# Retention and two matmul layers on one core: the decay moved from the chunks to the tokens

## The chip, the cores and the metric

One Trainium2 chip, one NeuronCore. The metric is the device time of one execution in microseconds, the median of several runs. The lower it is, the better.

## What is computed

The first part is attention with a decaying state, for 4 sequences of 768 tokens and 8 heads of width 64:

```python
gamma = 1.0 - 2.0 ** (-5.0 - np.arange(H))
for t in range(S):
    state = gamma * state + outer(k[t], v[t])      # 64 x 64 for each head
    y[t] = (1 / sqrt(D)) * q[t] @ state
x = y                                              # 3072 tokens x 512
h = ((x @ w1) * (x @ w2)) @ w3 @ w_out             # 512 -> 1024 -> 1024 -> 512
z = h @ w_in                                       # 512 -> 2048
out = (z * sigmoid(1.702 * z)) @ moe2_w_out        # 2048 -> 512
```

The weights arrive as float64 and q, k, v as float32. The output is float32, 3072 x 512.

## The kernel before

**Stage 0** (chunks) goes over 24 chunks of 128 tokens, six to a sequence. For a chunk, TensorE makes the scores k·q of all heads (L193, 8 matmuls, which the trace shows as 16 passes), VectorE multiplies them by a table that holds the causal mask, the decay and the scale (L217, two instructions, each for one head of every pair), and TensorE multiplies v by the result into the output y (L259). From the second chunk of a sequence on, TensorE adds the state times q (L269). q is scaled for that by GpSimd (L206). The state itself is renewed once in a chunk: GpSimd scales k by the decay to the end of the chunk (L209), TensorE multiplies it with v into PSUM (L228), GpSimd multiplies the old state by the decay of a whole chunk (L241), and VectorE adds the two (L247, two instructions on 64 partitions each; L251, a copy, in the first chunk of a sequence). ScalarE copies y to SBUF (L283) and issues its DMA to memory (L284). Of the first four chunks y stays on the chip, split into a high and a low part (L145 on ScalarE, L146 on VectorE).

**Weights** run beside this. A weight is loaded in 72 pieces of 128x512 float64 (512 KB), and `tick()` moves the pieces on by a step: it fetches pieces (L88, on SyncE's queue), and for three pieces at different stages ScalarE takes a scaled absolute value (L107), VectorE makes a float32 of the two words in four instructions (L110, L111, L112, L115), ScalarE rounds it to the high part (L103) and GpSimd subtracts to get the low part (L119). `TICKS` says how many steps a chunk takes: 1 in chunks 0 to 12, 2 in chunks 13 to 18, 1 in the last five. From chunk 12 on, TensorE also multiplies w3 by w_out, in halves of 12 matmuls (`mix`, `HALVES`: 16 halves in all); each second half ends in ScalarE and VectorE instructions (L303, L304).

**Stages 1 and 2** are the layers, over 6 blocks of 512 tokens. Every product is three matmuls (L129 to L131: high·high, high·low, low·high). In stage 1 a block has 8 steps f of 24 + 12 matmuls. Between the 24 and the 12, ScalarE copies one product (L382), VectorE multiplies it by the other (L383), ScalarE rounds (L364) and VectorE subtracts (L365). In the last four steps the next block is loaded and split (L145, L146). Block 0 takes two weight steps for each f (four at f = 0), block 5 two. Stage 2 has 16 steps of 24 matmuls; in its first block each has one weight step.

Each engine works through its instructions in the order in which the program issues them (`tc.manual_schedule()`). In a chunk c that is:

```python
load_qk(c + 2); load_kv(c + 2)
scale_qk(c + 1); scores(c + 1)
if HALVES[c] > 0: mix_half()
if TICKS[c] > 1: tick()
updates(c)
if HALVES[c] > 1: mix_half()
outputs(c); next_state(c)
masked(c + 1)
if TICKS[c] > 0: tick()
```

The PSUM tiles for y and for the state's update have one buffer each, those for the scores two each.

Of the kernel before, what the change touches and what calls it, by code (L numbers as in the profile page):

```python
# [7 lines left out]
F32 = mybir.dt.float32  # L8
# [3 lines left out]
ALU = mybir.AluOpType  # L12
# [24 lines left out]
def tile_kernel(  # L37
# [10 lines left out]
    cq: bass.AP,  # L48
    ck: bass.AP,
    cg: bass.AP,  # L50
# [39 lines left out]
    def tick():  # L90
        """A step of the weights' pieces, each of which is at another stage."""
# [26 lines left out]
        if 0 <= l < len(pieces):  # L118
            nc.gpsimd.tensor_tensor(lo, whole, hi.bitcast(F32), ALU.subtract)  # L119
# [31 lines left out]
    with tc.manual_schedule():  # L151
        with (
# [32 lines left out]
            sc, pt, qs, ks, us = {}, {}, {}, {}, {}  # L185

            def scores(c):
                pair = []
                for j in range(2):
                    t = ps0.tile([P, NP, P], F32, tag=f"s{j}", bufs=2, name=f"sc{j}")  # L190
                    r = slice(j * D, (j + 1) * D)
                    for p in range(NP):
                        nc.tensor.matmul(  # L193
                            t[:, p, :],
                            qkt[c][r, 1, p, :],
                            qkt[c][r, 0, p, :],
                            start=True,
                            stop=True,
                        )
                    pair.append(t)  # L200
# [20 lines left out]
            def updates(c):  # L221
                """What the chunk adds to the state."""
                if c % NCK == NCK - 1:
                    return
                us[c] = ps0.tile([P, NP, D], F32, tag="u", name="u")
                for p in range(NP):
                    for j in range(2):
                        nc.tensor.matmul(  # L228
                            us[c][j * D : (j + 1) * D, p, :],
                            ks[c][:, 2 * p + j, :],  # L230
                            kvt[c, 1][:, 2 * p + j, :],
                            start=True,
                            stop=True,
                        )

            def next_state(c):
# [15 lines left out]
                del us[c]  # L252

            def outputs(c):
                y = ps0.tile([P, NP, P], F32, tag="y", name="y")
                first = c % NCK == 0
                for p in range(NP):
                    for j in range(2):
                        nc.tensor.matmul(  # L259
                            y[j * D : (j + 1) * D, p, :],  # L260
                            kvt[c, 1][:, 2 * p + j, :],
# [5 lines left out]
                if not first:  # L267
                    for p in range(NP):
# [3 lines left out]
                            qs[c][:, p, :],  # L272
# [5 lines left out]
                t = slice(t0, t0 + P)  # L278
                if i == order[0]:
# [283 lines left out]
```

## Time and profile before

| | |
|---|---|
| time, median of 3 runs | 1127.29 us (1125.37 to 1127.29) |
| span of the profiled execution | 1124.6 us |
| TensorE busy | 1082.3 us, 96% of the span |
| VectorE busy | 540.0 us |
| ScalarE busy | 312.0 us |
| GpSimd busy | 164.0 us |
| mean granted TensorE clock | 0.988 |

The span runs from the first to the last instruction, and the profiled execution's own time is the span and a few microseconds around it. PE is TensorE, PEld its weight loads, DVE VectorE, ACT ScalarE, POOL GpSimd. "L112" is line 112 of the kernel. "Busy" counts an instruction from its start to its end, whatever it did in between.

### The profile page before, as it was taken

Reading aid. Unit: us, or ns where it says so; the run is one execution under the profiler, and the core shown is the slowest. Engines: PE = TensorE matmul, PEld = TensorE weight load, DVE = VectorE, ACT = ScalarE, POOL = GpSimd, SP = SyncE. Lnnn points to the kernel's source line nnn. Section 1 sums busy time; section 2 is a strip of 40 time slices with the busy share of each in tenths; the row PEclk is TensorE's granted clock in tenths of the full one; section 3 lists DMA queues with packets and bytes.
Section 4 is the critical chain, followed back from the end, with each engine's and each line's share of the span. In section 5 each row is a group of like instructions: output and inputs, shape, how many; then the busy total and the mean of one; then the engine's idle time right before and its main releaser. Section 6 shows DMA issues by size and latency. Waiting matters only on the chain.

```text
span 1124.6 us, 13473 instructions
## 1 busy us (share of the span) xinstructions
PE 1082.3 (96%) x5472; PEld 891.4 (79%) x5472; DVE 540.0 (48%) x744; ACT 312.0 (28%) x534; POOL 164.0 (15%) x134
## 2 busy tenths in 40 slices
PE   7879998998999999999998999999999999999998
PEld 6767777876888888888876888888888888888886
DVE  4999998994222222223897823223223223223222
ACT  1223323342122112212344423222223223223222
POOL 4666563320000000000322200000000000000000
PEclk9899999998999999999998999999999999999999
DMA  9887764432011010101443101002002001001001
GB/s 364 275 291 248 239 237 143 145 132 75 10 35 50 20 57 19 57 10 62 173 132 132 38 18 59 0 10 66 1 9 67 1 1 62 14 1 44 13 1 38
DMA packets 45183, 93.94 MB, mean 84 GB/s; under 512 B 4417, under 2 KB 14657, under 8 KB 45121
## 3 DMA queue, kind: packets, MB, share of 16 engines
q1 hardware_dynamic: 34560, 87.84, 22.8%
q10 hardware_dynamic: 10560, 5.24, 1.6%
q8 instruction: 43, 0.70, 0.2%
q14 instruction: 20, 0.16, 0.0%
HBM read 75.24 MB, written 17.83 MB: 83 GB/s over the span
## 4 chain that ended last, share of the span: by engine, by line
PE 76%; DVE 20%; issue 2%; ACT 1%; DMA 1%; ACTq 0%; DVEq 0%
PE psm L130 13%; PE psm L129 13%; PE psm L131 13%; PE acc L129 11%; PE acc L131 11%; PE acc L130 11%; DVE x L112 6%; DVE x L110 4%; DVE x L111 3%; DVE pt L217 2%; DVE x L115 2%; PE sc L193 1%; PE y L259 1%; DVE tmp L383 1%; PE y L269 1%
## 5 line engine op out<-in xcount | busy, mean ns | idle before, releaser
L129 PE MATMUL psm<-xh,wh 128*128 128x512 f32 x768 | 300.4, 391 | 8.3 <-ACT xh L145 8.3
L130 PE MATMUL psm<-xl,wh 128*128 128x512 f32 x768 | 300.3, 391 | 0.0
L131 PE MATMUL psm<-xh,wl 128*128 128x512 f32 x768 | 299.8, 390 | 0.0
L441 DVE TENSOR_TENSOR tmp<-tmp,psm 128x512 f32<-128x512 f32 x96 | 65.9, 686 | 262.5 <-ACT tmp L440 262.5
L129 PEld LDWEIGHTS psm<-xh,wh 128*128 128x128 f32 x768 | 144.9, 189 | 39.4 <-ACT xh L145 9.2
L130 PEld LDWEIGHTS psm<-xl,wh 128*128 128x128 f32 x768 | 144.7, 188 | 30.9 <-DVE xl L146 1.0
L131 PEld LDWEIGHTS psm<-xh,wl 128*128 128x128 f32 x768 | 144.9, 189 | 30.0
L119 POOL TENSOR_TENSOR wl<-x,wh 128x512 fp32r<-128x512 f32 x72 | 94.3, 1310 | 473.0 <-ACT wh L103 470.0
L364 ACT CAST hh<-tmp 128x512 fp32r<-128x512 f32 x144 | 89.3, 620 | 222.5 <-DVE tmp L383 130.1
L131 PE MATMUL acc<-wh,hl 128*128 128x512 f32 x384 | 149.5, 389 | 0.0
L129 PE MATMUL acc<-wh,hh 128*128 128x512 f32 x384 | 149.5, 389 | 0.0
L130 PE MATMUL acc<-wl,hh 128*128 128x512 f32 x384 | 149.4, 389 | 0.0
L365 DVE TENSOR_TENSOR hl<-tmp,hh 128x512 fp32r<-128x512 f32 x144 | 99.6, 692 | 98.9 <-ACT hh L364 98.9
L440 ACT ACTIVATE tmp<-psm 128x512 f32<-128x512 f32 x96 | 57.2, 596 | 272.9 <-PE psm L131 272.8
L383 DVE TENSOR_TENSOR tmp<-tmp,psm 128x512 f32<-128x512 f32 x48 | 32.9, 685 | 165.7 <-PE psm L131 165.7
L129 PEld LDWEIGHTS acc<-wh,hh 128*128 128x128 f32 x384 | 72.0, 188 | 15.3 <-ACT hh L364 0.4
L131 PEld LDWEIGHTS acc<-wh,hl 128*128 128x128 f32 x384 | 72.0, 188 | 15.3 <-DVE hl L365 0.4
L130 PEld LDWEIGHTS acc<-wl,hh 128*128 128x128 f32 x384 | 72.2, 188 | 14.9
L112 DVE SCALAR_TENSOR_TENSOR x<-raw,x 128x512 int32<-128x512 int32 x72 | 81.1, 1127 | 2.5
L129 PE MATMUL acc<-hh,wh 128*128 128x512 f32 x192 | 76.5, 399 | 4.1 <-ACT hh L364 4.1
L130 PE MATMUL acc<-hl,wh 128*128 128x512 f32 x192 | 76.6, 399 | 1.0 <-DVE hl L365 0.8
L131 PE MATMUL acc<-hh,wl 128*128 128x512 f32 x192 | 75.7, 394 | 0.0
(47 smaller groups left out, 967.8 us busy)
## 6 DMA issues: line engine op xcount, KB each, us to landing
raw<-in_w_dram SPq DMA_DIRECT2D x32, 512.0 KB, 4.4
qkt<-in_qk_dram SPq DMA_DIRECT2D x24, 512.0 KB, 6.5
raw<-in_wo_dram SPq DMA_DIRECT2D x24, 512.0 KB, 4.9
raw<-in_wi_dram SPq DMA_DIRECT2D x16, 512.0 KB, 3.7
k<-in_kv_dram SPq DMA_DIRECT2D x24, 256.0 KB, 6.2
v<-in_kv_dram SPq DMA_DIRECT2D x24, 256.0 KB, 6.1
yd<-st SPq DMA_DIRECT2D x24, 256.0 KB, 2.4
xr<-yd SPq DMA_DIRECT2D x24, 256.0 KB, 3.1
```

The lines of the kernel that those rows point to most:

```text
L110: nc.vector.tensor_scalar(x, x, LEAST, MOST, ALU.max, ALU.min)
L111: nc.vector.tensor_scalar(bits, bits, 3, None, ALU.logical_shift_left)
L112: nc.vector.scalar_tensor_tensor(bits, raw[:, :, 0], 29, bits, ALU.logical_shift_right, ALU.bitwise_or)
L119: nc.gpsimd.tensor_tensor(lo, whole, hi.bitcast(F32), ALU.subtract)
L129: nc.tensor.matmul(ps, wh, xh, start=start, stop=False, skip_group_check=True)
L130: nc.tensor.matmul(ps, wh, xl, start=False, stop=False, skip_group_check=True)
L131: nc.tensor.matmul(ps, wl, xh, start=False, stop=stop, skip_group_check=True)
L364: nc.scalar.copy(hi, t)
L365: nc.vector.tensor_tensor(lo, t, hi.bitcast(F32), ALU.subtract)
L383: nc.vector.tensor_tensor(t, t, pb, ALU.mult)
L440: nc.scalar.activation(t, ps, AF.Sigmoid, scale=ALPHA)
L441: nc.vector.tensor_tensor(t, t, ps, ALU.mult)
```

## The change

The decay is split into one factor for each key token, which goes onto v, and one for each query token, which goes onto y, both relative to the middle of the sequence. Then the state needs no decay of its own:

- v is multiplied by its factor on VectorE (`scale_v`); q and k are used as they come (L206 and L209 are gone).
- The mask holds only zeros and ones, the same for all heads (64 KB, where there were 512 KB).
- The updates of a sequence accumulate in one PSUM tile. ScalarE copies the two diagonal parts to SBUF after each chunk. GpSimd's product (L241) and VectorE's sum (L247, L251) are gone.
- y is multiplied by its factor on VectorE, into SBUF, where ScalarE copied it before. The factors come in six tables of 256 KB, one loaded in each of the first chunks.
- The low part of a weight piece is subtracted on VectorE.
- The scores of a pair's two heads alternate, where all first heads came before all second ones.
- The loads ahead of the first chunk come in another order.

```diff
         if 0 <= l < len(pieces):
-            nc.gpsimd.tensor_tensor(lo, whole, hi.bitcast(F32), ALU.subtract)
+            nc.vector.tensor_tensor(lo, whole, hi.bitcast(F32), ALU.subtract)
...
             load_qk(0)
-            mask = p0.tile([P, 2, NP, P], F32, name="mask")
+            mask = p0.tile([P, 1, P], F32, name="mask")
             nc.sync.dma_start(mask, cmask)
+            dv = p0.tile([P, NCK, H, 1], F32, name="dv")
+            nc.sync.dma_start(dv, cv)
+            load_kv(0)
             load_qk(1)
-            dk = p0.tile([P, H, 1], F32, name="dk")
-            nc.sync.dma_start(dk, ck)
-            load_kv(0)
-            dq = p0.tile([P, NP, P], F32, name="dq")
-            nc.sync.dma_start(dq, cq)
+            dy = []
+            def load_dy():
+                t = p0.tile([P, NP, P], F32, name=f"dy{len(dy)}")
+                nc.sync.dma_start(t, cy[:, len(dy)])
+                dy.append(t)
+            load_dy()
             load_kv(1)
-            gc = p0.tile([P, NP, 1], F32, name="gc")
-            nc.sync.dma_start(gc, cg)
...
             def scores(c):
...
-                for j in range(2):
-                    t = ps0.tile([P, NP, P], F32, tag=f"s{j}", bufs=2, name=f"sc{j}")
-                    r = slice(j * D, (j + 1) * D)
-                    for p in range(NP):
+                for p in range(NP):
+                    for j in range(2):
+                        r = slice(j * D, (j + 1) * D)
                         nc.tensor.matmul(
-                            t[:, p, :],
+                            pair[j][:, p, :],
...
-            def scale_qk(c):
-                if c % NCK:
-                    qs[c] = p0.tile([P, NP, P], F32, tag="qs", bufs=2, name="qs")
-                    nc.gpsimd.tensor_tensor(qs[c], qkt[c][:, 0], dq, ALU.mult)
-                if c % NCK < NCK - 1:
-                    ks[c] = p0.tile([P, H, D], F32, tag="ks", bufs=2, name="ks")
-                    nc.gpsimd.tensor_tensor(
-                        ks[c], kvt[c, 0], dk.to_broadcast([P, H, D]), ALU.mult
-                    )
+            def scale_v(c):
+                vs[c] = p0.tile([P, H, D], F32, tag="vs", bufs=3, name="vs")
+                nc.vector.tensor_tensor(
+                    vs[c],
+                    kvt[c, 1],
+                    dv[:, c % NCK].to_broadcast([P, H, D]),
+                    ALU.mult,
+                )
...
-                    nc.vector.tensor_tensor(t, sc[c][j], mask[:, j], ALU.mult)
+                    nc.vector.tensor_tensor(
+                        t, sc[c][j], mask.to_broadcast([P, NP, P]), ALU.mult
+                    )
...
             def updates(c):
-                us[c] = ps0.tile([P, NP, D], F32, tag="u", name="u")
+                if n == 0:
+                    us[i] = ps0.tile([P, NP, D], F32, tag="u", name="u")
                 for p in range(NP):
                     for j in range(2):
                         nc.tensor.matmul(
-                            us[c][j * D : (j + 1) * D, p, :],
-                            ks[c][:, 2 * p + j, :],
-                            kvt[c, 1][:, 2 * p + j, :],
-                            start=True,
+                            us[i][j * D : (j + 1) * D, p, :],
+                            kvt[c, 0][:, 2 * p + j, :],
+                            vs[c][:, 2 * p + j, :],
+                            start=(n == 0 and p == 0),
...
             def next_state(c):
                 new = state[(c + 1) % 2]
-                if c % NCK:
-                    nc.gpsimd.tensor_tensor(
-                        new, state[c % 2], gc.to_broadcast([P, NP, P]), ALU.mult
-                    )
                 for j in range(2):
                     r = slice(j * D, (j + 1) * D)
-                    if c % NCK:
-                        nc.vector.tensor_tensor(
-                            new[r, :, r], us[c][r], new[r, :, r], ALU.add
-                        )
-                    else:
-                        nc.vector.tensor_copy(new[r, :, r], us[c][r])
+                    nc.scalar.copy(new[r, :, r], us[c // NCK][r])
...
             def outputs(c):
...
-                            qs[c][:, p, :],
+                            qkt[c][:, 0, p, :],
...
+                x = p0.tile([P, KD, P], F32, tag="xb", bufs=3, name="xb")
+                nc.vector.tensor_tensor(x, y, dy[c % NCK], ALU.mult)
                 if i == order[0]:
-                    split(i, y, slice(None), t)
+                    split(i, x, slice(None), t)
                 else:
-                    x = p0.tile([P, KD, P], F32, tag="xb", bufs=3, name="xb")
-                    nc.scalar.copy(x, y)
                     nc.scalar.dma_start(xd[i][:, :, t], x)
...
                     load_kv(c + 2)
+                if len(dy) < NCK:
+                    load_dy()
                 if TICKS[c] > 2:
                     tick()
                 if c + 1 < NC:
-                    scale_qk(c + 1)
+                    scale_v(c + 1)
                     scores(c + 1)
```

## Rows read from the trace of the kernel before

**Rows 1.** Busy time of each engine in eight stretches of the span (start:end, length, then busy us and instructions of each engine, the mean granted TensorE clock, the DMA engines' busy share, and GB/s). The stretches are cut at the first mask product (L217) of chunks 1, 13 and 19, at TensorE's first matmul of stage 1, and where TensorE ends its two longest waits in the layers.

```profile
0.00:14.86 14.86, 9.65 (x80) 9.06 (x80) 2.83 (x6) 1.91 (x3) 6.77 (x11) 1.00 0.87 329
14.86:88.20 73.34, 60.05 (x637) 51.50 (x638) 68.49 (x92) 20.65 (x36) 43.66 (x36) 0.93 0.87 303
88.20:146.68 58.48, 52.43 (x420) 41.93 (x419) 57.04 (x75) 19.39 (x36) 33.44 (x27) 1.00 0.71 238
146.68:182.13 35.45, 35.12 (x304) 28.90 (x305) 33.09 (x44) 9.79 (x17) 20.73 (x16) 1.00 0.59 204
182.13:259.39 77.26, 68.58 (x288) 54.00 (x286) 68.99 (x90) 32.22 (x58) 23.50 (x18) 0.97 0.40 136
259.39:527.00 267.61, 267.60 (x1169) 220.99 (x1170) 69.43 (x102) 55.09 (x95) 3.98 (x3) 0.99 0.11 36
527.00:594.44 67.44, 62.69 (x274) 50.70 (x272) 57.97 (x77) 27.54 (x50) 18.92 (x14) 0.99 0.43 148
594.44:1124.60 530.16, 526.20 (x2307) 434.32 (x2307) 182.17 (x264) 145.39 (x245) 12.95 (x10) 1.00 0.09 29
```

**Rows 2.** TensorE's waits over the whole span, two of the list: the line that waited, for whom, us in total, times, the longest.

```profile
PE psm L129 <- ACT xh L145: 8.3, 2, 4.2
PE u L228 <- DVE state L247: 7.8, 7, 1.9
```

**Rows 3.** The timeline around 104 us, inside a chunk with two weight steps (start, length, engine, line): VectorE's instructions of the steps, and the GpSimd instruction beside them.

```profile
102.79 0.69 DVE L112 SCALAR_TENSOR_TENSOR x<-raw,x 128x512 int32<-128x512 int32 x1
103.51 0.69 DVE L115 SCALAR_TENSOR_TENSOR x<-raw,x 128x512 int32<-128x512 int32 x1
...
104.12 0.42 DVE L110 TENSOR_SCALAR x<-x 128x512 f32<-128x512 f32 x1
...
104.58 0.43 DVE L111 TENSOR_SCALAR x<-x 128x512 int32<-128x512 int32 x1
...
104.93 1.27 POOL L119 TENSOR_TENSOR wl<-x,wh 128x512 fp32r<-128x512 f32 x1 [2.47 <-ACT wh L103]
105.04 1.72 DVE L112 SCALAR_TENSOR_TENSOR x<-raw,x 128x512 int32<-128x512 int32 x1
```

**Rows 4.** Groups of instructions in the first 300 us, by line and shape (count, busy us, mean ns of one, idle before): VectorE's mask products, state sums and low parts, and ScalarE's copies of y.

```profile
L217 DVE TENSOR_TENSOR pt<-sc,mask 128x512 f32<-128x512 f32 x48 | 31.0, 686 | 7.7 <-PE sc L193 7.1
L247 DVE TENSOR_TENSOR state<-u,state 64x256 f32<-64x256 f32 x32 | 13.4, 418 | 1.2 <-POOL state L241 0.9
L365 DVE TENSOR_TENSOR hl<-tmp,hh 128x512 fp32r<-128x512 f32 x13 | 9.0, 692 | 8.9 <-ACT hh L364 8.9
...
L283 ACT COPY xb<-y 128x512 f32<-128x512 f32 x20 | 11.7, 582 | 41.5 <-PE y L269 36.6 <-PE y L259 4.9
```

**Rows 5.** The same timeline, the work of a chunk: y, the state's part of it, the scores, the first matmul of a half of the mix, ScalarE's issue of the DMA of y, and the update.

```profile
102.62 1.09 PE L259 MATMUL y<-pt,v 128*64 128x128 f32 x16
103.64 1.16 PE L269 MATMUL y<-qs,state 128*128 128x128 f32 x8
...
104.73 1.71 PE L193 MATMUL sc<-qkt 64*128 64x128 f32 x16
...
106.37 0.50 PE L129 MATMUL psw<-wh 128*128 128x512 f32 x1
106.42 0.52 ACTq L284 DMA_DIRECT2D xd<-xb  x1
...
109.82 0.69 PE L228 MATMUL u<-v,ks 128*64 128x64 f32 x16 [0.44 <-DVE state L247]
```

**Rows 6.** VectorE's product of the gate (L383) in stage 1, from its timeline: steps f = 0, 4 and 7 of block 0, and two neighbouring steps of block 1.

```profile
195.24 0.68 DVE L383 TENSOR_TENSOR tmp<-tmp,psm 128x512 f32<-128x512 f32 x1
...
229.83 0.68 DVE L383 TENSOR_TENSOR tmp<-tmp,psm 128x512 f32<-128x512 f32 x1
...
257.49 0.68 DVE L383 TENSOR_TENSOR tmp<-tmp,psm 128x512 f32<-128x512 f32 x1
...
282.22 0.69 DVE L383 TENSOR_TENSOR tmp<-tmp,psm 128x512 f32<-128x512 f32 x1 [6.09 <-PE psm L131]
290.38 0.69 DVE L383 TENSOR_TENSOR tmp<-tmp,psm 128x512 f32<-128x512 f32 x1 [6.09 <-PE psm L131]
```

**Rows 7.** VectorE's timeline in block 5 of stage 1: the end of step f = 3 with the instructions behind it, and the product of the last step, f = 7.

```profile
556.36 0.68 DVE L383 TENSOR_TENSOR tmp<-tmp,psm 128x512 f32<-128x512 f32 x1
557.72 0.69 DVE L365 TENSOR_TENSOR hl<-tmp,hh 128x512 fp32r<-128x512 f32 x1 [0.69 <-ACT hh L364]
558.33 0.42 DVE L110 TENSOR_SCALAR x<-x 128x512 f32<-128x512 f32 x1
...
592.53 0.68 DVE L383 TENSOR_TENSOR tmp<-tmp,psm 128x512 f32<-128x512 f32 x1
```

**Rows 8.** TensorE's timeline after its wait at the end of block 5: the first and the twelfth matmul.

```profile
594.44 0.79 PE L129 MATMUL psm<-xh,wh 128*128 128x512 f32 x1 [4.19 <-ACT xh L145]
...
599.49 0.39 PE L131 MATMUL acc<-hh,wl 128*128 128x512 f32 x1
```

**Rows 9.** The timeline of the first chunks: GpSimd's scaling of the second chunk's k, ScalarE's rounding of the first y, and VectorE's mask products of chunk 1.

```profile
10.68 1.05 POOL L209 TENSOR_TENSOR ks<-k,dk 128x512 f32<-128x512 f32 x1
...
12.75 0.58 ACT L145 CAST xh<-y 128x512 fp32r<-128x512 f32 x1 [10.73 <-PE y L259]
...
14.86 1.29 DVE L217 TENSOR_TENSOR pt<-sc,mask 128x512 f32<-128x512 f32 x2
```

More of the change, by code (lines that the diff above doesn't have):

```diff
@@ L47, in tile_kernel @@
     cmask: bass.AP,
-    cq: bass.AP,
-    ck: bass.AP,
-    cg: bass.AP,
+    cy: bass.AP,
+    cv: bass.AP,
     out: bass.AP,
@@ L183, in tile_kernel @@
                 nc.gpsimd.memset(s, 0.0)
-            sc, pt, qs, ks, us = {}, {}, {}, {}, {}
+            sc, pt, vs, us = {}, {}, {}, {}
             def scores(c):
-                pair = []
-                for j in range(2):
-                    t = ps0.tile([P, NP, P], F32, tag=f"s{j}", bufs=2, name=f"sc{j}")
-                    r = slice(j * D, (j + 1) * D)
-                    for p in range(NP):
+                pair = [
+                    ps0.tile([P, NP, P], F32, tag=f"s{j}", bufs=2, name=f"sc{j}")
+                    for j in range(2)
+                ]
+                for p in range(NP):
+                    for j in range(2):
+                        r = slice(j * D, (j + 1) * D)
                         nc.tensor.matmul(
-                            t[:, p, :],
+                            pair[j][:, p, :],
                             qkt[c][r, 1, p, :],
@@ L199, in scores @@
                         )
-                    pair.append(t)
                 sc[c] = pair
-            def scale_qk(c):
-                if c % NCK:
-                    qs[c] = p0.tile([P, NP, P], F32, tag="qs", bufs=2, name="qs")
-                    nc.gpsimd.tensor_tensor(qs[c], qkt[c][:, 0], dq, ALU.mult)
-                if c % NCK < NCK - 1:
-                    ks[c] = p0.tile([P, H, D], F32, tag="ks", bufs=2, name="ks")
-                    nc.gpsimd.tensor_tensor(
-                        ks[c], kvt[c, 0], dk.to_broadcast([P, H, D]), ALU.mult
-                    )
+            def scale_v(c):
[6 more added lines that the diff above has]
+                )
             def masked(c):
@@ L221, in updates @@
             def updates(c):
-                if c % NCK == NCK - 1:
+                i, n = divmod(c, NCK)
+                if n == NCK - 1:
                     return
-                us[c] = ps0.tile([P, NP, D], F32, tag="u", name="u")
+                if n == 0:
+                    us[i] = ps0.tile([P, NP, D], F32, tag="u", name="u")
                 for p in range(NP):
@@ L228, in updates @@
                         nc.tensor.matmul(
-                            us[c][j * D : (j + 1) * D, p, :],
-                            ks[c][:, 2 * p + j, :],
-                            kvt[c, 1][:, 2 * p + j, :],
-                            start=True,
+                            us[i][j * D : (j + 1) * D, p, :],
+                            kvt[c, 0][:, 2 * p + j, :],
+                            vs[c][:, 2 * p + j, :],
+                            start=(n == 0 and p == 0),
                             stop=True,
+                            skip_group_check=True,
                         )
@@ L239, in next_state @@
                 new = state[(c + 1) % 2]
-                if c % NCK:
-                    nc.gpsimd.tensor_tensor(
-                        new, state[c % 2], gc.to_broadcast([P, NP, P]), ALU.mult
-                    )
                 for j in range(2):
                     r = slice(j * D, (j + 1) * D)
-                    if c % NCK:
-                        nc.vector.tensor_tensor(
-                            new[r, :, r], us[c][r], new[r, :, r], ALU.add
-                        )
-                    else:
-                        nc.vector.tensor_copy(new[r, :, r], us[c][r])
-                del us[c]
+                    nc.scalar.copy(new[r, :, r], us[c // NCK][r])
             def outputs(c):
@@ L260, in outputs @@
                             y[j * D : (j + 1) * D, p, :],
-                            kvt[c, 1][:, 2 * p + j, :],
+                            vs[c][:, 2 * p + j, :],
                             pt[c][j][:, p, :],
@@ L306, in tile_kernel @@
             psw = None
-            scale_qk(0)
+            scale_v(0)
             scores(0)
@@ L495, in _constants @@
     t = np.arange(P, dtype=np.float64)
-    lag = t[None, :] - t[:, None]
-    scale = 1.0 / np.sqrt(D)
-    mask = np.where(lag >= 0, scale * g[:, None, None] ** np.maximum(lag, 0), 0.0)
-    cmask = mask.reshape(NP, 2, P, P).transpose(2, 1, 0, 3)
-    gq = scale * g[:, None] ** (t + 1)
-    cq = np.broadcast_to(gq.reshape(NP, 2, 1, P), (NP, 2, D, P))
-    cq = cq.transpose(1, 2, 0, 3).reshape(P, NP, P)
-    ck = (g[None, :] ** (P - 1 - t)[:, None]).reshape(P, H, 1)
-    cg = np.broadcast_to((g**P).reshape(NP, 2, 1), (NP, 2, D))
-    cg = cg.transpose(1, 2, 0).reshape(P, NP, 1)
-    return [np.ascontiguousarray(x, dtype=np.float32) for x in (cmask, cq, ck, cg)]
+    cmask = (t[None, :] >= t[:, None])[:, None, :]
+    at = (np.arange(NCK)[:, None] * P + t - S // 2)[:, :, None]
+    gy = g**at / np.sqrt(D)
+    cy = np.broadcast_to(
+        gy.reshape(NCK, P, NP, 2, 1).transpose(3, 4, 0, 2, 1), (2, D, NCK, NP, P)
+    )
+    cy = cy.reshape(P, NCK, NP, P)
+    cv = (g**-at).transpose(1, 0, 2).reshape(P, NCK, H, 1)
+    return [np.ascontiguousarray(x, dtype=np.float32) for x in (cmask, cy, cv)]
 def kernel(**inputs):
@@ L543 @@
     }
-    given.update(zip(("cmask", "cq", "ck", "cg"), _constants()))
+    given.update(zip(("cmask", "cy", "cv"), _constants()))
     nc = _bacc.Bacc("TRN2", target_bir_lowering=False, num_devices=1)
```

## The prediction, as it was put on record

> **What bounds the kernel now.** I read first the busy times by stretch, then TensorE's waits, then VectorE's timeline inside the stretches in which TensorE waits. From 259 to 527 us and from 594 us to the end TensorE is busy for 267.6 of 267.6 us and 526.2 of 530.2 us [rows 1]. The change can give nothing there by itself. The other stretches add up to 326.8 us, of which TensorE is busy for 288.5, and in four of them VectorE is nearly full: 68.5 of 73.3, 57.0 of 58.5, 33.1 of 35.5 and 69.0 of 77.3 us [rows 1]. So up to 259 us the order of the day is VectorE's, except from 147 to 182 us, where TensorE is busy for 35.1 of 35.5. From 527 to 594 us VectorE has 58.0 of 67.4, and TensorE's whole loss is one wait of 4.19 us at the end [rows 8]. The list of waits says the same: TensorE waits longest for a rounded part of the next block (8.3 us in two waits), which ScalarE can make only behind VectorE's product of the last step, and for VectorE's sum into the state (7.8 us) [rows 2].
>
> VectorE's busy time is not all work. One and the same instruction on L112 takes 0.69 us at 102.79 and 1.72 us at 105.04. The second began 0.11 us behind a GpSimd subtraction that ran from 104.93 to 106.20, and it ended 0.56 us after that one [rows 3]. It waited for GpSimd to be done and then did its work. L111 at 104.58, with no GpSimd instruction beside it, took 0.43 us [rows 3]. The mask products, which read PSUM, show no such lengthening: 686 ns on average over 48 [rows 4].
>
> **A weight step.** Undisturbed, from start to start, it takes 0.46 us (L110 to L111), 0.46 (L111 to L112), 0.72 (L112 to L115) and 0.61 (L115 to the next) [rows 3], together 2.25 us. The low part that moves in has the form of L365, 692 ns busy [rows 4] and 0.61 us from its start to the next start [rows 7]. So a step of five instructions takes 2.86 us. What does one of four take today? From f = 0 to f = 4 of block 0 four intervals take 34.59 us, 8.65 each [rows 6]. Each holds two steps, the gate's product to its low part (1.36 us) and the low part (0.61) [rows 7]. That leaves 6.68 us, 3.34 for a step. With one instruction more, but GpSimd silent, a step gets cheaper by 0.48 us.
>
> **A chunk.** VectorE loses the two sums (0.42 us each [rows 4]) and gets the factors on v and on y, each like a low part, 0.61 us. Its mask products stay at 1.2 us for two; a table repeated over the heads I price as before. With one weight step that makes 1.2 + 0.61 + 0.61 + 2.86 = 5.28 us, with two 8.14, and 0.61 more where a product of the mix ends. In the first four chunks 1.3 us come on top, since the split of y waits for ScalarE (0.69) and then subtracts (0.61).
>
> What moves to ScalarE is a new chain. ScalarE works in order, so the two copies of the state stand behind the issue of y's DMA (0.52 us [rows 5]), which now waits for VectorE's factor on y. And the next update waits for the copies, as they read its PSUM tile. From one y to the next: factor 0.69, issue 0.52, two copies of 64x256, update 0.62, y 1.02, the state's part 1.09 (the last three from start to start [rows 5]). A copy of 256 elements has no row. Half of L283's 582 ns [rows 4] bounds it below and the whole above; I take 0.37, nearer to the half. Five handovers at up to 0.1 us make the chain 5.2 us, with bounds of 4.6 and 5.6. The scores fit into it, while TensorE waits. Also behind the copies on ScalarE stand the high part and the absolute value of the weight step. VectorE needs them only in that step's last instruction and in the next step, and so they are covered by its 2.25 us of the other four. If the copies were late by more than that, VectorE would stand, and with it the mask products behind it.
>
> DMA: the stretch from 14.9 to 88.2 us moves 303 GB/s at a share of 0.87 [rows 1], 348 GB/s if it were full. Its 22.2 MB and five tables of 0.26 MB would then take 67.6 us.
>
> **The sum, by stretch.** *Before 14.86 us.* The first y waits for v and the mask; VectorE now scales v of chunk 1 before it touches y, so that chunk's loads set the time. Today GpSimd begins on chunk 1's k at 10.68 us [rows 9]; the loads up to v of that chunk make 2.8 MB. In the new order they make 2.4 MB, and at the same rate v of chunk 1 is there at about 9.4. Scaling it, the factor on y, ScalarE's rounding (today at 12.75 [rows 9]) and the low part bring the mask products from 14.86 to 12.1: -2.8 us (bounds 0 and -3.5).
>
> *To 88.20, 12 chunks.* VectorE's floor is 12 x 5.28 + 3 x 1.3 = 67.3 us, the chain's 12 x 5.2 + 3.9 = 66, DMA's 67.6. Three limits so close together don't overlap without loss; I take 70.0 for 73.34, -3.3 us (bounds 0 and -6).
>
> *To 146.68, 6 chunks.* VectorE 8.75, 8.14, 8.75 and 8.14 us in four; in the two with two halves of the mix TensorE: scores 1.64, 24 matmuls at 8.16 / 36 = 0.227 [rows 6], update 0.62, y 2.11, together 9.8. The sum is 53.4 for 58.48, -5.1 us (bounds -1, if the chain comes on top, and -7).
>
> *To 182.13.* TensorE is full. What is left is the order of the scores. Their passes take 0.10 us, and their weight loads stay as wide as they are. Nearest is their own row, so I take 0.4 us for the three chunks here. The other bound is y's: its 16 passes, on alternating halves, take 1.02 us where the scores' 16 take 1.64 [rows 5], so 0 to -1.9 us.
>
> *To 259.39, block 0.* From TensorE's start at 182.13 VectorE needs the factor on the last y and four steps until the first gate product: 12.1 us, where it is 13.1 today [rows 6]. Then four intervals of 2 x 2.86 + 1.97 = 7.69 and three of 8.29 (0.6 for the low part of the next block's split), 55.6 us, where they are 34.59 + 27.66 = 62.25 [rows 6]. From the last product to the end of the wait it stays 1.9 us (259.39 less 257.49). Together 69.6 instead of 77.26: -7.6 us. TensorE has 285 matmuls up to that point, 64.7 us, and still some 2 us of waiting for the first product, so 67 at least: bounds of -10 and, if a step gets cheaper by only a fifth of a us, -3.
>
> *To 527.* TensorE is full: 0.
>
> *To 594.44, block 5.* VectorE's last product comes at 592.53; from 556.36 [rows 7] there were one interval without a split and three with one, and as many before. At 7.69 and 8.29 it comes at about 586.5, and the rounded part 1.9 us after it, 588.4. TensorE without its wait is there at 590.25. The wait goes: -4.2 us (bounds 0 and -4.2). VectorE is then behind TensorE by nothing that TensorE feels.
>
> *Behind it.* After that wait the first and the twelfth matmul start 5.05 us apart [rows 8], where eleven spacings of 0.227 make 2.5. They run at the lower level of TensorE's clock, 1.2 GHz, and without the wait they would not: -2.5 us (bounds 0 and -2.5). After 259 us the same happens, and I leave it, since a wait of 2 to 3 us stays there.
>
> ScalarE's other instructions, the dropped copy of y and GpSimd's absence cost nothing: ScalarE has 20 of 73 us in its fullest chunk stretch [rows 1].
>
> The sum is -2.8 - 3.3 - 5.1 - 0.4 - 7.6 - 4.2 - 2.5 = -25.9 us on the span of 1124.6. The median of the runs is 2.7 us above that span, and I set the same difference behind: 1127.3 - 25.9 = 1101.4 us. Half of it is the layers', where only the weight step matters, and half the chunks'.
>
> **Rivals.** *The chunks keep their pace* (0.20). The chain over ScalarE, or loads that come late, take what VectorE gives back. For it: three limits within 2 us over 12 chunks, and VectorE now itself waits for v, with all behind it. Against it: from 88 us on DMA has a share of 0.71 [rows 1]. Then only block 0, block 5 and what follows them are left, 14.3 us: 1113.
>
> *The clock falls in the chunks* (0.07), and this one ends slower. In each chunk TensorE now waits for ScalarE's copies, about 1 to 2 us. Its clock in this stretch is 0.93 on average already [rows 1], and after 4.19 us of rest it ran at half [rows 8]. At 1.2 GHz update, y and the state's part take 5.5 us instead of 2.7, and the chain 8 us, 1.9 more than today's 6.1 for a chunk. Over the 12 chunks that is +22, which outdoes the 14.3 of the layers: 1135. It decides from a chain of 7.3 us (6.1 + 14.3 / 12), that is a mean granted clock below about 0.6 to 88 us. Against it: today's waits there are as long (up to 1.9 us), and the clock is above 0.9.
>
> *The long L110 to L112 don't come from GpSimd* (0.03). Then 72 low parts and 24 factors are added to a VectorE that stays slow: +31 us in the chunks and +10 in each of blocks 0 and 5, 1175. Rows 3 speak clearly against it.
>
> *The scores run in twos* (0.10). By rows 5 alternating halves can bring 16 passes from 1.64 to 1.02 us; halved, they give 0.82 us in each of the five chunks that TensorE sets, 4.1 us for my 0.4, and with block 0 at TensorE's own 67 us (2.6 more) the time is 1095. The Trainium skill, TensorEngine Tiling (Array Packing), Theoretical Speedup, has up to a factor of 2 for a contraction of 64 or less. By that rule it is 1098 from the scores alone; no row of this case shows two row halves at work at once.
>
> *No change* (0.03): the chunks lose what the layers win.
>
> **The numbers.** The forecast has 0.57, with a range of its own of 1094 to 1109. With most of the rival at 1113 and the upper bounds of the terms, 8 times in 10 the time lies between 1092 and 1116. A difference under 0.2% (2.3 us) could not be told from none. Faster 0.87, same 0.03, slower 0.10.
>
> **What would show it.** L110, L111 and L112 at 0.43, 0.43 and 0.69 us throughout; VectorE's intervals in block 0 near 7.7 and 8.3 us; a wait of 2 to 3 us after block 0 and none after block 5; the mask products of chunk 13 near 82 us and of chunk 19 near 136. I am wrong if chunks with one step take 6 us or more, with VectorE or TensorE waiting for a copy of the state or a load; if the clock in the chunks is below 0.9; or if low parts wait for ScalarE's rounding, which would make a step longer than 2.86 us.

## The result and the profile after

The changed kernel takes 1096.46 us (median of 4 runs, 1096.32 to 1096.69), where the kernel before took 1127.29 (1125.37 to 1127.45) beside it. The ratio is 0.9725, with a 95% interval of 0.9711 to 0.9738. So it is faster by 30.8 us, where 25.9 were forecast, and the time lies in the range. Its span is 1094.8 us, 29.8 less than before.

The page's first line of the changed kernel answers to the table of before: GpSimd has nothing left but its setting of constants, and VectorE, with 80 instructions more, is busy for 37 us less.

```profile
PE 1057.8 (97%) x5472; PEld 871.7 (80%) x5472; DVE 502.6 (46%) x824; ACT 319.2 (29%) x554; POOL 1.2 (0%) x6
```

The stretches of the changed kernel, cut at the same events as in [rows 1] (start:end, length, then busy us and count for PE, PEld, DVE, ACT, POOL, the granted clock, the DMA share, GB/s). The seventh begins inside step f = 0 of block 5. No long wait marks its end any more, and the cut lies 0.15 us behind the matmul that answers to the one of before:

```profile
0.00:15.59 15.59, 7.77 (x80) 6.88 (x80) 3.88 (x6) 2.51 (x4) 1.19 (x6) 1.00 0.84 311
15.59:81.98 66.39, 50.99 (x637) 42.52 (x637) 60.68 (x107) 21.90 (x44) 0.00 (x0) 0.95 0.93 335
81.98:132.98 51.00, 47.72 (x422) 38.09 (x420) 49.77 (x89) 20.91 (x38) 0.00 (x0) 1.00 0.86 295
132.98:167.42 34.44, 32.94 (x304) 26.96 (x305) 27.47 (x48) 12.04 (x24) 0.00 (x0) 1.00 0.60 209
167.42:237.23 69.81, 65.45 (x288) 53.34 (x286) 62.19 (x110) 32.59 (x57) 0.00 (x0) 1.00 0.45 147
237.23:504.34 267.11, 266.80 (x1169) 220.50 (x1170) 68.00 (x106) 55.10 (x95) 0.00 (x0) 0.99 0.12 36
504.34:566.10 61.76, 61.76 (x274) 51.01 (x272) 52.31 (x92) 28.60 (x51) 0.00 (x0) 1.00 0.50 162
566.10:1094.80 528.70, 524.40 (x2308) 432.39 (x2306) 178.34 (x273) 145.52 (x245) 0.00 (x0) 1.00 0.09 29
```

Against [rows 1], stretch by stretch, in us:

| stretch | forecast | measured |
|---|---|---|
| up to the mask products of chunk 1 | -2.8 | +0.7 |
| to chunk 13 | -3.3 | -7.0 |
| to chunk 19 | -5.1 | -7.5 |
| to stage 1 | -0.4 | -1.0 |
| block 0 | -7.6 | -7.5 |
| blocks 1 to 4 | 0 | -0.5 |
| block 5 | -4.2 | -5.7 |
| behind it | -2.5 | -1.5 |
| sum | -25.9 | -29.8 |

A whole one-step chunk of VectorE in the changed kernel's timeline (L109 to L114 are the old L110 to L115, L118 the low part, L209 the factor on v, L278 the factor on y, L220 the mask products):

```profile
45.48 0.42 DVE L109 TENSOR_SCALAR x<-x 128x512 f32<-128x512 f32 x1
...
45.94 0.43 DVE L110 TENSOR_SCALAR x<-x 128x512 int32<-128x512 int32 x1
...
46.40 0.69 DVE L111 SCALAR_TENSOR_TENSOR x<-raw,x 128x512 int32<-128x512 int32 x1
...
47.12 0.69 DVE L114 SCALAR_TENSOR_TENSOR x<-raw,x 128x512 int32<-128x512 int32 x1
47.73 0.69 DVE L118 TENSOR_TENSOR wl<-x,wh 128x512 fp32r<-128x512 f32 x1
48.33 0.68 DVE L209 TENSOR_TENSOR vs<-v,dv 128x512 f32<-128x512 f32 x1
...
48.94 0.68 DVE L278 TENSOR_TENSOR xb<-y,dy 128x512 f32<-128x512 f32 x1
49.54 1.28 DVE L220 TENSOR_TENSOR pt<-sc,mask 128x512 f32<-128x512 f32 x2
50.73 0.42 DVE L109 TENSOR_SCALAR x<-x 128x512 f32<-128x512 f32 x1
```

No instruction is drawn out any more, where [rows 3] have 1.72 us beside GpSimd. The step takes 2.85 us from start to start (45.48 to 48.33), with 2.86 forecast, and the chunk 5.25 (45.48 to 50.73), with 5.28 forecast. There is no gap: VectorE sets the pace.

TensorE's waits in the changed kernel, three of the list, answer to [rows 2]. The wait after block 5 is gone, the one after block 0 has shrunk from 4.16 to 1.6 us, and the wait for the state goes to ScalarE now and has doubled:

```profile
PE u L235 <- ACT state L250: 16.5, 11, 3.2
PE sc L198 <- DMA qkt<-in_qk_dram: 7.9, 5, 4.3
...
PE psm L128 <- ACT xh L144: 1.6, 1, 1.6
```

### The profile page after: what moved, and what is told of

It reads as the page before. It is cut to its first block, busy times and chain, and to the rows that moved or that the text cites. A ratio compares the mean times of both kernels' runs of the same rounds, so it can differ in the third digit from the quotient of the medians.

```text
span 1094.8 us, 13310 instructions
## 1 busy us (share of the span) xinstructions
PE 1057.8 (97%) x5472; PEld 871.7 (80%) x5472; DVE 502.6 (46%) x824; ACT 319.2 (29%) x554; POOL 1.2 (0%) x6
## 4 chain that ended last, share of the span: by engine, by line
PE 75%; DVE 16%; DMA 5%; issue 2%; ACT 1%; SPq 0%; DVEq 0%; ACTq 0%
PE psm L129 13%; PE psm L130 13%; PE psm L128 13%; PE acc L130 11%; PE acc L128 11%; PE acc L129 11%; DVE x L111 3%; DVE wl L118 3%; DMA qkt<-in_qk_dram 2%; DVE x L110 2%; DVE x L114 2%; DVE x L109 2%; DVE pt L220 1%; ACT hh L364 1%; DMA xd<-xb 1%
## 5 line engine op out<-in xcount | busy, mean ns | idle before, releaser
L383 DVE TENSOR_TENSOR tmp<-tmp,psm 128x512 f32<-128x512 f32 x48 | 32.9, 686 | 166.5 <-PE psm L130 166.5
L102 ACT CAST wh<-x 128x512 fp32r<-128x512 f32 x72 | 44.6, 620 | 49.4 <-DVE x L114 35.7
L382 ACT COPY tmp<-psm 128x512 f32<-128x512 f32 x48 | 28.0, 583 | 105.0 <-PE psm L130 105.0
```

The source lines that it names most:

```text
L102: nc.scalar.copy(hi, whole)
L382: nc.scalar.copy(t, pa)
L383: nc.vector.tensor_tensor(t, t, pb, ALU.mult)
```

## The experiments

The theory is that of the prediction: VectorE waited for GpSimd, a weight step without GpSimd is cheaper although it has one instruction more, VectorE sets the pace of the chunks and of blocks 0 and 5, and the new chain over ScalarE is hidden behind it. The first two runs part this from the rival that the new form of the decay brought the gain. The runs on the order of the scores and on the state's copies part it from the rivals that this order or the chain sets the chunks. The others test what still bounds the kernel.

**The low parts on GpSimd again**, all else as changed:

```diff
-            nc.vector.tensor_tensor(lo, whole, hi.bitcast(F32), ALU.subtract)
+            nc.gpsimd.tensor_tensor(lo, whole, hi.bitcast(F32), ALU.subtract)
```

> The changed kernel with one part undone: the low part of a weight piece is subtracted on GpSimd again, nothing else is on GpSimd. Theory (VectorE waited for GpSimd, and a weight step gets cheaper without it although it holds one instruction more): the intervals of the gate's product in block 0 go back from 7.68 and 8.29 us to 8.65 and 9.22, the wait after block 5 comes back, and one-step chunks take 5.2 to 5.8 us, since the one subtraction of a step can delay VectorE by up to 1.3 us where VectorE saves 0.61. The layers give back some 14 us: 1109 to 1116 us. Rival (the GpSimd products of q, k and the state were what slowed VectorE, and the low part on VectorE is a burden): VectorE is lighter by 0.61 us for each of 72 steps, block 0 is TensorE's at 67 us, 1090 to 1096 us.

Measured: 1121.7 us, a ratio of 0.9943 (0.9926 to 0.9961) to the kernel before, whose median beside it was 1128.57. This one instruction for each step, moved back, takes 24 us of the gain. In this kernel's timeline both engines wait for each other: this subtraction of GpSimd takes 1.77 us instead of 1.27 [rows 3], and VectorE's L114 beside it 1.64 instead of 0.69.

```profile
106.65 0.69 DVE L111 SCALAR_TENSOR_TENSOR x<-raw,x 128x512 int32<-128x512 int32 x1
106.69 1.77 POOL L118 TENSOR_TENSOR wl<-x,wh 128x512 fp32r<-128x512 f32 x1 [5.00 <-DVE x L110]
107.38 1.64 DVE L114 SCALAR_TENSOR_TENSOR x<-raw,x 128x512 int32<-128x512 int32 x1
```

The gate's products of block 0 are back at 8.64 us for four intervals and 9.22 for three, and TensorE's wait for the split is back at its old length:

```profile
190.92 0.68 DVE L383 TENSOR_TENSOR tmp<-tmp,psm 128x512 f32<-128x512 f32 x1
...
225.48 0.68 DVE L383 TENSOR_TENSOR tmp<-tmp,psm 128x512 f32<-128x512 f32 x1
...
253.14 0.68 DVE L383 TENSOR_TENSOR tmp<-tmp,psm 128x512 f32<-128x512 f32 x1
```

```profile
PE psm L128 <- ACT xh L144: 8.3, 2, 4.2
```

So the theory's mechanism holds, and the rival (1090 to 1096 us) falls. The time lies above the expected 1116, since I had counted only the layers: the chunks, too, become slower, by 3.9, 3.9 and 1.6 us in their three stretches.

**The low parts on VectorE alone**, in the kernel before, with the same line changed the other way:

> The kernel before with one part of the change alone: the low part of a weight piece on VectorE, the decay as it was, with q, k and the state scaled on GpSimd. Theory: the layers gain what they gained in the changed kernel (block 0's intervals 7.68 and 8.29 us, no wait after block 5, 14 us in all), and the chunks, where three GpSimd products of about 1.25 us each are left in 6 us, gain little or lose up to 5 us: 1108 to 1118 us. Rival (most of the gain comes from the decay's new form, in the chunks): block 0 stays near 77 us and the time at 1122 us or above.

Measured: 1105.78 us, ratio 0.9803 (0.9783 to 0.9823). Its stretches from chunk 1 to 13, from 13 to 19 and block 0:

```profile
15.30:87.18 71.88, 58.34 (x640) 50.17 (x641) 67.45 (x101) 21.50 (x36) 33.57 (x28) 0.95 0.89 309
87.18:143.30 56.12, 50.55 (x417) 40.86 (x415) 54.68 (x86) 20.42 (x35) 17.94 (x14) 1.00 0.74 248
...
178.76:248.09 69.33, 67.54 (x289) 54.64 (x287) 61.58 (x109) 33.40 (x59) 0.00 (x0) 0.98 0.44 149
```

Block 0 gains all that it gains in the changed kernel. The chunks gain 1.5 and 2.4 us, although three GpSimd products are left in each, so the time is 2 us below what I expected. By spans, low parts alone give -20.7 us (1103.9), the rest of the change alone (the decay's new form, the order of the scores and of the loads), which is the run before this one, -5.3 (1119.3), and both together -29.8. The layers' gain is the low parts' alone: with them on GpSimd, what follows TensorE's start of stage 1 takes 942.5 us, as before. In the chunks each part is worth more with the other: TensorE starts stage 1 at 182.1 us before, at 178.8 with the low parts alone, at 176.8 with the rest alone, and at 167.4 with both. Only when both are gone from GpSimd is VectorE never held up. In the whole time this surplus is 3.8 us by the spans of one execution each and 2.4 by the ratios, and their intervals leave it open whether it is there.

**The scores in the old order**:

```diff
-                for p in range(NP):
-                    for j in range(2):
+                for j in range(2):
+                    for p in range(NP):
```

> The changed kernel with the scores in the old order, all first heads before all second ones. In the changed kernel 16 passes take 1.16 us instead of 1.71. Theory (VectorE sets the one-step chunks, TensorE only the chunks with two halves of the mix and the last five): the 16 passes go back to 1.71 us, one-step chunks stay at 5.25 us, and 0.55 us come back in five to seven chunks: 2.5 to 4 us more, 1099 to 1100.5 us. Rival (the order of the scores carried the chunks' whole surplus over the forecast, in each of 24 chunks): 10 to 13 us more, 1107 to 1110 us. If it is 1096 to 1097, the order was worth nothing.

Measured: 1100.31 us (1097.42 to 1103.76), ratio 0.9751 (0.9724 to 0.9779), hard to tell from 0.9725. Two lines, the first of the changed kernel, the second of this one, show 16 passes of the scores:

```profile
97.85 1.16 PE L198 MATMUL sc<-qkt 64*128 64x128 f32 x16
```

```profile
141.68 1.71 PE L198 MATMUL sc<-qkt 64*128 64x128 f32 x16
```

The passes do what was expected of them. The stretch from chunk 13 to 19 takes 51.03 us, with the new order 51.00: nothing there hangs on the scores. From chunk 19 to stage 1 it takes 36.1 us for 34.4, the 0.55 us of three chunks. But the stretch from chunk 1 to 13 was 3.5 us longer, all of it in one chunk, in which the scores waited for a load and VectorE then for y:

```profile
78.19 2.30 PE L198 MATMUL sc<-qkt 64*128 64x128 f32 x16 [2.10 <-DMA qkt<-in_qk_dram]
...
85.97 0.69 DVE L278 TENSOR_TENSOR xb<-y,dy 128x512 f32<-128x512 f32 x1 [3.41 <-PE y L257]
```

Whether that belongs to the order of the scores took a second run, with the changed kernel itself beside it.

> The changed kernel, unaltered, on one chip with the scores in the old order. Time 1095.5 to 1097.5 us; stretches as in its first profile: chunk 1 to 13 in 66 to 67 us, chunk 13 to 19 in 51.0, from there to stage 1 in 34 to 37 us, depending on whether the clock falls behind the 3 us for which TensorE waits for the state's copy in chunk 19.

> The scores in the old order a second time. In the first profile one chunk of the one-step stretch took 8.75 us, since TensorE's scores waited 2.10 us for a load and half a mix stood behind them. If that is the loads' lateness and falls by chance, the stretch from chunk 1 to 13 takes 66 to 67 us now, as in the changed kernel, and only 1.6 us of the last five chunks and about 1 us of the first are left: 2 to 3.5 us more than the changed kernel beside it. If it belongs to the order of the scores, the stretch takes 69 to 70.5 us again: 5 to 7 us more.

Measured: the changed kernel 1097.11 us, ratio 0.9717 (0.9698 to 0.9737), stretches of 66.3, 51.0 and 34.4 us. The old order 1097.97 us, ratio 0.9719 (0.9703 to 0.9734), with 66.9, 51.0 and 36.1 us, and the mask products of chunk 1 at 16.71 us for 15.45. The same kernel did without the long chunk this time, so that one was a late load and not the scores. Stage 1 begins 3.6 us later with the old order, within the 2.5 to 4 that I had expected of the time, though by another way: 1.3 us in the head, 0.6 to chunk 13, nothing to chunk 19 and 1.7 behind it. But the time does not tell the two apart: their spans differ by 1.9 us, and their ratios by 0.0002. The other 1.6 us came back by TensorE's clock. In block 0 TensorE waits 2.53 us for the first rounded product in both runs. Here are the 10 us around that wait and the 10 us around the end of block 0, first of the changed kernel, then with the old order:

```profile
179.10:189.10 10.00, 8.09 (x34) 6.49 (x35) 8.42 (x16) 4.78 (x9) 0.00 (x0) 1.00 0.42 147
...
234.99:244.99 10.00, 8.10 (x28) 6.03 (x27) 6.14 (x12) 3.92 (x7) 0.00 (x0) 0.83 0.01 2
```

```profile
182.65:192.65 10.00, 8.09 (x27) 6.33 (x28) 8.42 (x16) 4.79 (x9) 0.00 (x0) 0.83 0.41 150
...
238.53:248.53 10.00, 9.70 (x42) 7.47 (x41) 6.70 (x12) 3.94 (x7) 0.00 (x0) 1.00 0.09 33
```

In the changed kernel the clock stayed up behind the first wait, TensorE reached the end of the block early, waited there for 1.6 us, and ran at the lower level after that. With the old order the clock fell behind the first wait, where VectorE sets the pace and the loss costs nothing, and stayed up at the end. From TensorE's start of stage 1 to the first gate product of block 1 that is 75.8 us in both profiles of the changed kernel, and 74.2 in both with the old order. The rival with its 10 to 13 us falls.

**The state's copies first**:

```diff
-                outputs(c)
                 next_state(c)
+                outputs(c)
```

> The changed kernel with the copies of the state issued ahead of y's part, so that on ScalarE they no longer stand behind the DMA issue that waits for VectorE's factor on y. TensorE's waits of 16.5 us for these copies should go. Theory (the chain over ScalarE is hidden behind VectorE's 5.25 us of a chunk): one-step chunks stay at 5.25 us and the time within 2 us of the changed kernel's, 1094.5 to 1097 us. Rival (the chain sets the pace): chunks get shorter, and most of the 16.5 us are gained, 1081 to 1089 us.

Measured: 1093.93 us, ratio 0.9696 (0.9673 to 0.972), which overlaps that of the changed kernel. The waits for the state are gone, and TensorE waits for VectorE's mask products instead (first view, from the list of waits). The chunks keep their pace: the stretch from chunk 13 to 19 (second view) took 51.00 us in the changed kernel, and the stretch before it takes 66.15 us here for 66.39:

```profile
PE y L257 <- DVE pt L220: 12.7, 12, 1.9
```

```profile
81.71:132.70 50.99, 48.37 (x436) 38.53 (x434) 49.76 (x90) 20.55 (x38) 0.00 (x0) 1.00 0.82 286
```

The chain over ScalarE is hidden, as forecast. 16.5 us of waits were worth about 1 us at the start of stage 1. The span is 2.6 us shorter; the other 1.6 are the clock's in block 0, as with the old order of the scores (74.2 us for 75.8).

**Another order of the first loads**:

```diff
             nc.sync.dma_start(dv, cv)
-            load_kv(0)
             load_qk(1)
+            load_kv(0)
+            load_kv(1)
...
             load_dy()
-            load_kv(1)
```

> The changed kernel with another order of its first loads: q and k of chunk 1 come ahead of k and v of chunk 0 again, and the first table for y last. In the changed kernel TensorE's scores of chunk 1 stand in its queue ahead of chunk 0's update and y, and wait 2.54 us for their q and k until 8.97 us; y of chunk 0 starts at 11.88 and the mask products of chunk 1 at 15.59 us. Theory (the scores of chunk 1, moved behind, hold up y of chunk 0): the scores start before 8 us and the mask products of chunk 1 at 13.5 to 14.8 us, the time 0.8 to 2 us shorter. Rival (VectorE's wait for v of chunk 1, at 10.95 us, sets the head whatever the order): the mask products of chunk 1 stay at 15.3 to 15.9 us, the time within 0.5 us of 1096.5.

Measured: 1095.81 us (1094.03 to 1098.5), ratio 0.9708 (0.9686 to 0.9731). The head of the changed kernel, from its timeline:

```profile
8.97 2.08 PE L198 MATMUL sc<-qkt 64*128 64x128 f32 x16 [2.54 <-DMA qkt<-in_qk_dram]
...
10.95 0.69 DVE L209 TENSOR_TENSOR vs<-v,dv 128x512 f32<-128x512 f32 x1 [1.27 <-DMA v<-in_kv_dram]
...
11.88 1.68 PE L257 MATMUL y<-pt,vs 128*64 128x128 f32 x16
...
15.59 1.28 DVE L220 TENSOR_TENSOR pt<-sc,mask 128x512 f32<-128x512 f32 x2
```

And the same places with the loads in the other order:

```profile
6.81 2.08 PE L198 MATMUL sc<-qkt 64*128 64x128 f32 x16 [0.43 <-DMA qkt<-in_qk_dram]
...
9.82 2.25 PE L257 MATMUL y<-pt,vs 128*64 128x128 f32 x16
...
14.10 1.28 DVE L220 TENSOR_TENSOR pt<-sc,mask 128x512 f32<-128x512 f32 x2
```

The head gets 1.5 us shorter, as the theory has it. At chunk 13 0.85 us of that are left, and in the end nothing that the time could show: in this execution TensorE's clock fell in chunk 19 (below), which cost 2.6 us. In block 0 it fell as with the old order of the scores, which gave back 1.6.

**Two weight steps fewer in block 0**:

```diff
-                    while n == 0 and ticks < 33 + 2 * f:
+                    while n == 0 and ticks < 31 + 2 * f:
...
-                    while n == 0 and ticks < 34 + 2 * f:
+                    while n == 0 and ticks < 32 + 2 * f:
...
-                    if last or (n == 2 and f == 1):
+                    if last or (n == 1 and f < 3):
```

> The changed kernel with two weight steps fewer in block 0: one before the first gate product, where there are three, and two at the start of block 1 in their place. Theory (block 0 is VectorE's: its first product stands behind four steps, and then seven intervals of 7.68 and 8.29 us follow): the first product comes 5.7 us earlier, TensorE becomes the limit with 285 matmuls, 65 us, and the stretch from its first matmul of stage 1 to the first of block 1 that waits for the last split takes 65 to 66.5 us instead of 69.8; without that wait of 1.6 us the clock does not fall behind it, 2 us more: 5 to 6.5 us in all, 1090 to 1091.5 us. Rival (TensorE's own pace sets block 0 already): 1095 to 1097 us.

Measured: 1088.68 us (1088.54 to 1088.85), ratio 0.9643 (0.9628 to 0.9659). The first gate product comes 6.6 us after TensorE's start of stage 1 instead of 12.3, and TensorE has no gap in all of block 0, nor a fall of its clock behind it:

```profile
166.68:190.00 23.32, 23.32 (x106) 19.32 (x105) 20.38 (x36) 10.54 (x19) 0.00 (x0) 1.00 0.44 146
190.00:230.00 40.00, 40.00 (x178) 33.15 (x177) 35.78 (x63) 18.69 (x33) 0.00 (x0) 1.00 0.45 146
230.00:240.00 10.00, 10.00 (x45) 8.10 (x44) 6.03 (x10) 4.05 (x9) 0.00 (x0) 1.00 0.15 54
```

Block 0 of the changed kernel was VectorE's. From TensorE's start of stage 1 to the gate's first product of block 1 it is 68.5 us for 75.8, a gain of 7.3, above the 5 to 6.5 that I gave it: 5.7 of the earlier first product and 1.6 of the clock.

**The three edits together**:

> The three edits together on the changed kernel: copies of the state first, the other order of the first loads, two weight steps fewer in block 0. If each gives what it should alone (0 to 2, 1 to 2, and 5 to 6.5 us): 1087 to 1090 us. If block 0 is TensorE's already, 1094 to 1096.

Measured: 1088.77 us, ratio 0.9639 (0.9617 to 0.9661). State and loads add nothing that could be measured to the steps in block 0. The chunks remain VectorE's: the stretch from chunk 13 to 19 takes 51.0 us. In this execution a load came late in chunk 2, and the stretch from chunk 1 to 13 took 68.6 us.

**And two steps fewer in the chunks**, on top of the three:

```diff
-TICKS = (1,) * 13 + (2,) * 6 + (1,) * 5
+TICKS = (1,) * 13 + (2,) * 4 + (1,) * 7
...
-                    while n == 0 and ticks < 31 + 2 * f:
+                    while n == 0 and ticks < 30 + 2 * f:
...
-                    while n == 0 and ticks < 32 + 2 * f:
+                    while n == 0 and ticks < 31 + 2 * f:
...
-                    if last or (n == 1 and f < 3):
+                    if last or (n == 1 and f < 4):
```

> As the three edits together, and chunks 17 and 18 with one weight step instead of two, so that the chunks hold 28 steps and block 0 fifteen or so, the rest in block 1. Theory (VectorE sets the chunks with two steps, 8.1 to 8.7 us each): these two chunks become TensorE's, at 6.6 and 9 us, and 3 to 5 us are gained on top of the three edits: 1083 to 1086 us. Rival (TensorE or the loads set the pace there): within 1 us of the three edits together.

Measured: 1085.92 us (1084.65 to 1088.25), ratio 0.9621 (0.9601 to 0.9642). The stretch from chunk 13 to 19 goes from 51.0 to 45.3 us, two steps of 2.85 less. TensorE is busy for nearly all of it, but VectorE has no gap either, and the two chunks take VectorE's 5.85 and 5.25 us, not the 6.6 and 9 that I expected of TensorE:

```profile
80.00:125.30 45.30, 45.00 (x412) 36.30 (x411) 44.27 (x80) 18.07 (x34) 0.00 (x0) 1.00 0.90 313
```

Part of it goes to block 0, which takes 66.95 us here, with a wait of 1.1 us at its end. The span is 4.6 us below that of the three edits. The two ratios' intervals overlap, so this last gain is shown by the trace alone. This is the fastest version, 1% below the changed kernel and 3.8% below the one before.

## Why the prediction was right, step by step

**A weight step** was sized to the hundredth: 2.86 us forecast, 2.85 measured, and the gate's intervals 7.68 and 8.29 us for 7.69 and 8.29. That VectorE waited for GpSimd is shown by the run that puts the low parts back and by the one that moves them alone.

**Block 0** came out at -7.5 us for -7.6, with the forecast wait at its end, 1.6 us long and not 2 to 3. **Block 5 and behind**: -7.1 us for -6.7, without the long wait, as forecast. Single terms are off: block 5 gained 1.5 us more, as the kernel before had further short waits in its last steps, and what follows 1 us less, since TensorE has short waits there now, the longest of 0.40 us.

**To chunk 13** the forecast was 70.0 us and 66.4 came. The failing step is VectorE's own sum of 67.3. It gives every chunk a whole weight step, but the first chunk of the stretch has none and the second none of the low part, 3.5 us less: 63.8. A loss of the size that I added for three limits lying close together, 2.7 us above that sum, did come: VectorE waited 1.7 us for y in the first chunk of the stretch and 0.9 in the seventh. The DMA engines had a share of 0.93 there, and in this execution no load held up VectorE. In two others a late load did, in one chunk each, for 3.5 and about 2 us.

**To chunk 19** the failing step is TensorE's 9.8 us for a chunk with two halves of the mix. The scores had nothing to do with it: with 1.71 us for them the stretch is the same. TensorE ends the chunk before, which holds one half, ahead of VectorE, and brings that lead into the long chunk: it is at the next scores at 87.48 us, where VectorE's mask products of the long chunk start at 90.68. Its load must be summed over neighbouring chunks: 8 halves at 2.72 and six chunks at 4.37 are 48 us, below VectorE's 51.

**The scores** were priced at their own row, 0.4 us for three chunks or 0.13 for 16 passes, with 0.62 as the other bound; 0.55 came, near the bound that y's passes gave. The Trainium skill, TensorEngine Tiling (Array Packing), Theoretical Speedup, has up to a factor of 2 for a contraction of 64 or less; the trace has 1.71 / 1.16, a factor of 1.5. The effect on the time was small, since the order counts only in the head and in the last chunks before stage 1.

**The head** was forecast at -2.8 us and was +0.7. Two steps failed. V of chunk 1 came at 10.95 us and not at 9.4. The row that I scaled, GpSimd's at 10.68 [rows 9], shows no arrival: GpSimd waited for nothing there, as its instruction before ran from 9.46 for 1.27 us. Nor did the rate stay the same: up to 16 us the DMA moved 313 GB/s, where it was 335 before. And I had looked only at VectorE's queue: on TensorE the scores of chunk 1 stand ahead of chunk 0's update and y, and it was their q and k that the new order of the loads had moved behind. With them back in front 1.5 us of the 3.5 return. What the rest hangs on was not tried.

**The chain over ScalarE**, whose copies took 0.367 us (0.37 forecast), is hidden: taking its waits away changed no chunk. Of the rivals, the chunks' pace, the clock (0.95 on average in the one-step chunks) and a VectorE that stays slow did not occur. The time lies nearer to the 1095 us of the rival on the scores than to the 1101.4 of the forecast, but not by that rival's way: the chunks with two halves do not hang on the scores, and block 0 took 69.8 us and not TensorE's own 67.

Part of the agreement is luck. The head came out 3.5 us longer than forecast and the stretch behind it 3.6 shorter, so that the mask products of chunk 13 start at 81.98 us, near the 82 of the forecast. The layers gave 15.1 us for 14.3, term by term; the chunks with their head gave 14.7 for 11.6, by terms of which three were wrong. (That ScalarE is fullest where it has 20 of 73 us was misread: it has 19.39 of 58.48 in the next stretch [rows 1]. It changes nothing.)

## What to carry to other kernels

If an instruction's length on VectorE varies beside GpSimd's work, price the move by VectorE's undisturbed rows: here an engine with 97% of the stretch from chunk 13 to 19 took on 14 instructions more in it, 89 for 75, and became faster. A wait that has grown, as that for the state did, is worth nothing while another engine is without a gap. Where a load is moved, look through every queue for what now waits for it, with all that stands behind it. And take a load's arrival from an instruction that waited for it.

## What the runs showed of the hardware

VectorE and GpSimd hold up each other. With one GpSimd subtraction left in a step, GpSimd's took 1.42 us on average and up to 1.80, for 1.31 before. All four other instructions of a step, on VectorE, were drawn out where they began inside it: those with one operand in SBUF (L109 up to 1.54 us, L110 up to 1.41) as well as those with two (L111 up to 1.79, L114 up to 1.67). The mask products, which read PSUM, kept 0.69 us each beside GpSimd [rows 4]. So did the factors on y, but they never ran beside it.

TensorE's clock doesn't answer equally to equal waits. In block 0 a wait of 2.5 us left the granted clock of the next stretch at 1.00 in both profiles of the changed kernel, and at 0.83 in four others (both with the old order of the scores, the state's copies first, the other loads). What decides it is open. In chunk 19 of the changed kernel TensorE waited 3.14 us and then made y and the state's part at a granted clock of 1.00 (134.48 to 139.33 us):

```profile
134.48 0.69 PE L235 MATMUL u<-vs,k 128*64 128x64 f32 x16 [3.14 <-ACT state L250]
135.00 1.04 PE L257 MATMUL y<-pt,vs 128*64 128x128 f32 x16
135.97 1.16 PE L267 MATMUL y<-qkt,state 128*128 128x128 f32 x8
```

With the other order of loads the wait was 3.11 us, and the same matmuls ran at 0.50, the lower level (133.65 to 138.50 us):

```profile
133.65 1.12 PE L235 MATMUL u<-vs,k 128*64 128x64 f32 x16 [3.11 <-ACT state L250]
134.56 1.92 PE L257 MATMUL y<-pt,vs 128*64 128x128 f32 x16
136.41 2.08 PE L267 MATMUL y<-qkt,state 128*128 128x128 f32 x8
```

That cost some 2.6 us in this stretch (37.1 us for 34.4), as much as the edits that these runs were to tell apart.
